# Channel mixer: the first products get priority over the second products everywhere, and attention runs 15 instead of 18 units ahead

## Chip, cores, metric

One core of a Trainium2 chip. The metric is the device time of one execution in microseconds, lower is better. A kernel is run several times and the median is quoted. Ratios are the mean time of one kernel's fast runs over the mean of the other's fast runs of the same rounds, so they are not quite the ratio of the quoted medians.

## The reference

Attention with a block mask, then a ResMLP block on its output. The matrices that matter here:

```python
# 4 batches, 8 heads, 768 tokens, head size 64, so d_model = 512; all scaled and masked as usual
x   = attention(q, k, v, mask)            # (4, 768, 512)
a1  = alpha1 * x + beta1
u   = x + lam * einsum('ts,bsd->btd', w_tok, a1)          # token mixer
a2  = alpha2 * u + beta2
out = u + lam * (maximum(a2 @ w_ch1, 0) @ w_ch2)          # channel mixer, 512 -> 2048 -> 512
```

`a2 @ w_ch1` are the *first products*, the product with `w_ch2` the *second products*. `lam` is about 0.01.

## The kernel before

The kernel is written as a list of jobs. A small list scheduler runs while the program is built. It puts each job on an engine in the order that its own estimates suggest, and that order is then fixed: every engine works through its list and waits wherever its next instruction isn't ready. So a job's priority (its third argument, the smaller the earlier) changes no work, only the order of instructions.

```python
# this kernel's PSUM buffers, in banks: sps 2 x 2 (scores), mm 2 x 1, cp 1, ops 1
slots = dict(sps=2, mm=2, cp=1, ops=1, eT=NET, head=NQB, vext=NV, ld=NLD, rel=3, ...)

for kk in range(2 * B):                       # a half batch (384 tokens) each
    relus = []
    for f in range(16):                       # first products: 16 groups of 4 matmuls, 384 columns
        # c1: hp[:, 0:384] += w1b[:, dk, f-th 128].T @ uT[:, dk, half]    for dk in 0..3
        # rl: hts[kk][:, f, :] = relu(hp + b1)  on ACT or DVE; frees the mm buffer
        deps = [ut_jobs[b * NPAIR + n] for n in range(NPAIR)] + b1_jobs
        take = ((("mm", "sps"), ("mmsel", kk, f)),) + (("hts",) if f == 0 else ())
        j = Job("PE", mmt(4, HS), (5, kk, f), c1, deps, take=take, ...)
        jr = Job(("ACT", "DVE"), 600.0, (0, kk, f), rl, [j], give=(("mmsel", kk, f),))
        relus.append(jr)
    for mi, (m, lo, w) in enumerate(parts):   # second products: per 128 tokens 4 pieces of 4 matmuls
        for r in range(4):
            deps = relus[4 * r : 4 * r + 4] + w2_jobs[2 * r : 2 * r + 2] + ([prev] if prev else [])
            take = ... ("cp", "ops") ...      # one accumulator; ops and sps only after attention
            prev = Job("PE", mmt(4, w), (6 if kk == 2 * B - 1 else 4, kk, mi, r), c2, deps, take=take, ...)
        # otf (DVE): ot = x_sb + cp, frees cp;  store (SP): ot to memory
...
def gated(j):      # a score job may run at most LEAD units ahead of the channel mixer;
                   # a unit is one of the nine steps in which a head pair's scores are made
    return j.gate is not None and j.gate >= NS and j.gate - NS > st["ch"] / rate + LEAD
...
if e == "PE" and not st["ch2"]:
    fill(t - free_at[e] - 60.0)               # until the first second product: filler matmuls in planned holes
```

Also on TensorE are the scores (of the first six head pairs one head at a time, later two heads of 64 rows at once), the value products into the bank `ops`, and the token mixer into `mm`. On DVE are the normalisation of each head (`x_sb`, which frees `ops`), masking, the copies of v (`vext`), and the additions.

The softmax here doesn't subtract the row's maximum and nothing guards it: scores larger than these inputs give would overflow.

## Time and profile before

| | before |
|---|---|
| median of 4 runs | 318.59 us (318.51 to 319.05) |
| span in the profile | 317.3 us |
| PE / DVE / ACT busy | 97% / 66% / 64% |
| last matmul ends | 313.8 us |

In the views PE stands for TensorE's matmuls and PEld for its weight loads, DVE for VectorE, ACT for ScalarE, POOL for GpSimd and SP for the engine that issues stores and transposing DMAs; PEclk is the clock granted to TensorE in 40 slices of the time, where 9 means 90% of full speed or more. From the page of the kernel before, first the busy time of the engines and the granted clock, then groups of instructions: line, engine, operation, output and inputs, shapes, count, then busy us, mean ns of one, idle us before them.

```profile
PE 307.4 (97%) x3234; PEld 189.6 (60%) x3269; DVE 208.8 (66%) x432; ACT 204.6 (64%) x262; POOL 51.2 (16%) x91
...
PEclk9999999999999999999999999999999999999999
...
L973 ACT ACTIVATE hts<-mm,b1t 128x384 bf16<-128x384 f32 x92 | 53.6, 583 | 59.8 <-PE mm L962 57.3
L962 PE MATMUL mm<-uT,w1b 128*128 128x384 bf16 x472 | 90.5, 326 | 0.6
L1007 PE MATMUL cp<-w2b,hts 128*128 128x512 bf16 (+1 forms) x307 | 75.8, 373 | 1.5
...
L977 DVE TENSOR_SCALAR hts<-mm,b1t 128x384 bf16<-128x384 f32 x26 | 16.0, 617 | 14.5 <-PE mm L962 14.5
```

ACT waits for TensorE's first products (57 us), not the other way round: TensorE is full. But 97% busy says little about what is left to win. A first product "takes" 326 ns on the page, and yet in the trace one starts every 162 ns. Products overlap, so a hole of 0.2 us between two of them shows up as hardly any idle time (0.6 us for all of L962). The holes have to be read from the start times of single records. Here are those around 122 us, where three groups of first products stand in a row (start in us, then the distance to the next start in ns):

```
122.127  163     second group
122.290  162
122.452  436     <- 274 ns longer than the others
122.888  162     third group, into the mm buffer that the first group used
123.050  162
```

The timeline of the kernel before around that place (start, duration, engine and line, out<-in, count):

```profile
121.31 2.39 PE L962 MATMUL mm<-uT,w1b 128*128 128x384 bf16 x12
121.35 1.02 ACT L780 ACTIVATE eT<-sps 128x1024 f16<-128x1024 f32 x1
...
122.25 1.15 ACT L973 ACTIVATE hts<-mm,b1t 128x384 bf16<-128x384 f32 x2
```

The first group ends its stream at 121.97. Its ReLU starts only at 122.25, behind an exponential, and takes 0.58 us. Until it has read the buffer the third group can't start. Ten such places after 85 us cost 0.10 to 0.27 us each, together 2.04 us. In all ten the first product of the held group starts 49 to 52 ns after the end of a ReLU; seven of these ReLUs run on DVE and three on ACT.

What PE itself waits for, in the view of waits of the kernel before (us in total, times, longest):

```profile
PE cp L171 <- DVE warm L166: 1.2, 1, 1.2
PE ops L716 <- DVE x_sb L651: 1.0, 1, 1.0
PE sps L676 <- ACT eT L691: 0.6, 1, 0.6
PE sps L676 <- ACT qx L238: 0.5, 1, 0.5
PE mm L427 <- DVE kx L281: 0.4, 1, 0.4
```

All but the second lie in the first 45 us, ahead of anything that the change touches. The second is at 69 us; the timeline there (in brackets: idle time before it and what ended it):

```profile
69.26 0.36 DVE L834 COPY vext<-v 128x768 f16<-128x768 f16 x1 [1.21 <-DMA v<-in_v_dram]
...
69.54 0.19 DVE L648 RECIPROCAL rcp<-ops 128x6 f32<-128x6 f32 x1
69.76 0.56 DVE L651 TENSOR_TENSOR x_sb<-ops,rcp 128x384 f32<-128x384 f32 x1
...
70.38 0.54 PE L716 MATMUL ops<-vext,eT 128*128 128x65 f16 x12 [1.00 <-DVE x_sb L651]
```

DVE's list has the copy of the eighth pair's v ahead of a normalisation that was ready. The v load landed late, DVE stood still for 1.2 us, and TensorE paid 1.0 us. (The view of waits counts from modelled ends and shows a little less than the start times do: this wait is 1.17 us by them.)

One more caution in reading: some matmul records are missing from this trace (3234 are there). A gap that is exactly one product longer than usual (216 ns before a second product) is a missing record, not a wait.

### The profile page before, as it was taken

The numbers are of one execution on the slowest core, as the hardware profiler recorded it, in microseconds if no ns is written. First come the engines' busy times: TensorE is split into PE (matmuls) and PEld (weight loads), VectorE is DVE, ScalarE is ACT, GpSimd is POOL, SyncE is SP. The second block draws the span as 40 slices with busy tenths as digits, with TensorE's granted clock in tenths as the row PEclk, the third lists the DMA queues.
The fourth block names the chain that finished last, engine by engine and source line by source line (L and its number), as shares of the span: only waits on it lengthen the run. The fifth ranks groups of instructions, "written<-read, shape, count | busy, mean of one in ns | idle before, by whom it ended". The sixth has DMA issues, their size and how long they took to land.

```text
span 317.3 us, 7694 instructions
## 1 busy us (share of the span) xinstructions
PE 307.4 (97%) x3234; PEld 189.6 (60%) x3269; DVE 208.8 (66%) x432; ACT 204.6 (64%) x262; POOL 51.2 (16%) x91
## 2 busy tenths in 40 slices
PE   7999999989999999999999999999999999999995
PEld 3677868865655555555656565555656565555544
DVE  4558988978778786978888786878777650201001
ACT  4999889987785666656765667657775526253620
POOL 4647170000221121122131121120000000000000
PEclk9999999999999999999999999999999999999999
DMA  6999999991544865436454744346100300201001
GB/s 148 184 254 201 211 202 215 176 161 30 78 73 74 140 72 95 84 77 116 62 92 82 135 81 89 75 82 110 28 3 33 92 8 19 101 0 66 35 33 66
DMA packets 47210, 30.81 MB, mean 97 GB/s; under 512 B 27552, under 2 KB 43080, under 8 KB 47176
## 3 DMA queue, kind: packets, MB, share of 16 engines
q0 software_dynamic: 15984, 15.47, 31.1%
q1 hardware_dynamic: 30940, 14.61, 20.5%
q8 instruction: 25, 0.41, 0.5%
q10 hardware_dynamic: 252, 0.24, 0.3%
q14 instruction: 9, 0.07, 0.1%
HBM read 32.04 MB, written 6.33 MB: 121 GB/s over the span
## 4 chain that ended last, share of the span: by engine, by line
PE 74%; DMA 13%; issue 5%; POOL 4%; DVE 2%; ACT 1%; POOLq 0%
PE mm L962 23%; PE cp L1007 22%; DMA v<-in_v_dram 9%; PE ops L812 8%; PE sps L754 7%; PE mm L889 7%; PE ops L1007 4%; DMA wtk<-in_moe_w_tok_dram 3%; PE sps L962 2%; POOL k L317 1%; DVE hts L977 1%; POOL q L317 1%; DMA q2f<-in_q_dram 1%; POOL v L317 1%; POOL w2b L390 1%
## 5 line engine op out<-in xcount | busy, mean ns | idle before, releaser
L780 ACT ACTIVATE eT<-sps 128x1024 f16<-128x1024 f32 x90 | 88.3, 1020 | 29.2 <-PE sps L754 28.3
L973 ACT ACTIVATE hts<-mm,b1t 128x384 bf16<-128x384 f32 x92 | 53.6, 583 | 59.8 <-PE mm L962 57.3
L962 PE MATMUL mm<-uT,w1b 128*128 128x384 bf16 x472 | 90.5, 326 | 0.6
L1007 PE MATMUL cp<-w2b,hts 128*128 128x512 bf16 (+1 forms) x307 | 75.8, 373 | 1.5
L785 DVE TENSOR_TENSOR eT<-eT,maskT 128x1024 f16<-128x1024 f16 x90 | 60.6, 686 | 13.2 <-ACT eT L780 12.8
L962 PEld LDWEIGHTS <-w1b 128*128 128x128 bf16 x512 | 47.2, 98 | 35.4 <-issue 5.1
L1007 PEld LDWEIGHTS <-hts 128*128 128x128 bf16 x400 | 36.6, 98 | 33.3 <-issue 0.3
L691 ACT ACTIVATE eT<-sps 128x1024 f16<-128x1024 f32 (+1 forms) x55 | 52.3, 1016 | 4.6 <-PE sps L676 4.3
L1024 DVE TENSOR_TENSOR ot<-x_sb,cp 128x512 f32<-128x512 f32 (+1 forms) x21 | 14.1, 673 | 44.9 <-PE cp L1007 40.6
L812 PEld LDWEIGHTS <-eT 128*128 128x128 f16 x720 | 29.1, 97 | 16.3 <-issue 5.9
L889 PE MATMUL mm<-a1p,wtokT 128*128 128x128 bf16 x576 | 36.8, 219 | 0.0
L812 PE MATMUL ops<-vext,eT 128*128 128x65 f16 x720 | 35.2, 194 | 0.0
L889 PEld LDWEIGHTS <-wtokT 128*128 128x128 bf16 x576 | 33.3, 98 | 2.2
L676 PE MATMUL sps<-qx,kx 88*128 88x512 bf16 (+1 forms) x144 | 31.5, 324 | 1.3 <-ACT eT L691 0.6
L315 POOL COPY held<-flag 1x1 bf16<-1x1 bf16 x24 | 8.3, 348 | 137.6 <-DVE flag L335 137.6
L754 PE MATMUL sps<-qx,kx 64*128 64x512 bf16 (+1 forms) x240 | 27.3, 326 | 0.0
L977 DVE TENSOR_SCALAR hts<-mm,b1t 128x384 bf16<-128x384 f32 x26 | 16.0, 617 | 14.5 <-PE mm L962 14.5
L716 PEld LDWEIGHTS <-eT 128*128 128x128 f16 x432 | 19.0, 97 | 6.7 <-DVE x_sb L651 1.7
L716 PE MATMUL ops<-vext,eT 128*128 128x65 f16 x432 | 21.0, 193 | 1.0 <-DVE x_sb L651 1.0
L899 DVE TENSOR_TENSOR x_sb<-x_sb,mm 128x384 f32<-128x384 f32 x32 | 17.6, 551 | 5.5 <-PE mm L889 5.4
L651 DVE TENSOR_TENSOR x_sb<-ops,rcp 128x384 f32<-128x384 f32 x32 | 17.8, 557 | 1.1
L905 DVE TENSOR_TENSOR ub<-x_sb,a_bc 128x384 bf16<-128x384 f32 x32 | 17.3, 553 | 0.2
(71 smaller groups left out, 226.6 us busy)
## 6 DMA issues: line engine op xcount, KB each, us to landing
out_dram<-ot SPq DMA_DIRECT2D x23, 256.0 KB
v<-in_v_dram POOLq DMA_DIRECT2D x16, 192.0 KB, 5.0
q<-in_q_dram POOLq DMA_DIRECT2D x15, 192.0 KB, 3.6
k<-in_k_dram POOLq DMA_DIRECT2D x15, 192.0 KB, 4.0
w1b<-in_moe_w_ch_dram POOLq DMA_DIRECT2D x4, 512.0 KB, 10.2
w2b<-in_moe_w_ch_dram POOLq DMA_DIRECT2D x4, 512.0 KB, 13.2
wtk<-in_moe_w_tok_dram POOLq DMA_DIRECT2D x3, 384.0 KB, 10.4
maskT<-mask_rows SPq DMA_DIRECT2D x14, 72.0 KB
```

Of the source, the lines that this page charges most:

```text
L676: nc.tensor.matmul(sps[:, f - u * UN : f - u * UN + w], kx[h][0:KC, ts(jt, P)], qx[h][0:KC, c : c + w], start=True, stop=True,)
L691: nc.scalar.activation(eT[:, c], sps[:, c], AF.Exp, bias=EXPB, scale=SCALE)
L716: nc.tensor.matmul(ops[p, a][:, t * VW : t * VW + D + 1], eTs[p, u][:, ts(i - u * GU, P)], vx[:, a, jt, 0 : D + 1], start=(i % HT == 0), s ...
L754: nc.tensor.matmul(sps[:, a * 512 + lo : a * 512 + lo + w], kx[sl][r, ts(jt, P)], qx[sl][r, c : c + w], start=True, stop=True,)
L780: nc.scalar.activation(eT[:], sps[:], AF.Exp, bias=EXPB, scale=SCALE)
L785: nc.vector.tensor_tensor(out=e, in0=e, in1=maskT[:, u, :].unsqueeze(1).broadcast_to([P, 2, 512]), op=ALU.min,)
L812: nc.tensor.matmul(ops[p, a][:, t * VW : t * VW + D + 1], eTs[p, u][:, a * 512 + c * P : a * 512 + (c + 1) * P], vx[:, a, jt, 0 : D + 1], ...
L889: nc.tensor.matmul(tp[:, j, :], wtokT[:, s, ts(3 * g + j, P)], tl["a1p", p][:, s, :], start=(s == 0), stop=(s == NT - 1),)
L962: nc.tensor.matmul(hp[:, 0:HS], w1b[:, dk, ts(f, P)], uTs[b][:, dk, ts(hf, HS)], start=(dk == 0), stop=(dk == 3),)
L973: nc.scalar.activation(hts[kk][:, f, :], hp[:, 0:HS], AF.Relu, bias=b1t[:, f : f + 1], scale=1.0)
L977: nc.vector.tensor_scalar(out=hts[kk][:, f, :], in0=hp[:, 0:HS], scalar1=b1t[:, f : f + 1], scalar2=0.0, op0=ALU.add, op1=ALU.max,)
L1007: nc.tensor.matmul(cps[kk, mi][:, 0:w], hts[kk][:, nk, ts(m, P)], w2tile[0][:, nk, lo : lo + w], start=(nk == 0), stop=(nk == 15),)
```

## The change

Second products shall only fill spots in which TensorE would wait. First products keep priority 5, and all second products get 6; before, that held only for the last half batch, and the others had 4. Attention's lead over the channel mixer goes from 18 to 15 units.

```diff
-LEAD = 18
+LEAD = 15
@@ first products
             deps = [ut_jobs[b * NPAIR + n] for n in range(NPAIR)] + b1_jobs
+            if f:
+                deps.append(first)
             ...
             j.ch = True
+            if not f:
+                first = j
@@ second products
-                prev = Job("PE", mmt(4, w), (6 if kk == 2 * B - 1 else 4, kk, mi, r), c2, deps, take=take,
+                prev = Job("PE", mmt(4, w), (6, kk, mi, r), c2, deps, take=take,
```

The dependency on `first` makes sure that the group that takes the `hts` buffer comes first. Built without it, the changed kernel failed in the scheduler (a ReLU looked for a buffer that didn't exist yet).

## The prediction

> **What bounds the kernel.** TensorE, by streaming. The page has PE busy 97% of 317.3 us, which alone proves little: it counts filler products, and the Trainium skill ("Trainium Kernel Development and Optimization", Performance Expectations) calls matmul busy time a bad metric because matmuls are pipelined. I read start-to-start times from the trace's matmul records: 162 ns for 384 columns, 216 for 512, 56 for 128. The skill's "TensorE: Matmul & The Clock Gate" (section on 56 ns, not 53.3) gives columns / 2.4 GHz + about 2.5 ns: 162.5, 215.8, 55.8. The trace agrees, clock granted 1.0. From 71 us to the last product (313.8 us) TensorE streams almost without a hole. The waits view has PE matmuls waiting 3.7 us in total. Entering and leaving a 64-row score block costs about 96 + 93 ns, 45 times, in both orders.
>
> Holes after 60 us: (a) ten of 0.10 to 0.27 us, 2.0 us in sum, where a third first product in a row needs one of two "mm" PSUM buffers whose ReLU isn't done (650 ns per group; ReLU 583 ns on ACT, 617 on DVE, plus drain); (b) 1.0 us at 69.4 us: a value product held by a normalisation that stood behind a late v load (DVE waited 1.2 us for it); (c) fillers of 0.1 to 0.4 us between 63 and 76 us. Other gaps are exactly one product long (216 ns): missing records.
>
> **What changes.** Matmuls, ReLUs and additions are the same but one filler (47 becomes 46, about 0.2 us). Only order moves: first products earlier, second ones as filler; attention held to 15, not 18, units ahead. ACT (64%) and DVE (66%) have slack off the critical path.
>
> **Costed from the two instruction orders and the pitches above.** Products that need an mm buffer freed less than 0.8 us of TensorE work before: 11 before, 4 after. At 0.22 us each (0.1 at milder ones) waits fall from 2.0 to 0.8 us: gain 1.2 to 1.5. Filler: gain 0.2. The wait at 69 us: 18 mixing products now stand ahead of it, but the late v load still delays DVE: gain 0 to 0.5. Against it: second products share one cp bank during attention, freed by a 0.67 us addition after the drain. Between two groups the old order left at least 1.29 us; the new leaves 0.75 twice and 1.04 once: loss 0.5 to 0.9. After the last token mix 28 second products (6.0 us) cover the path to the transposed u, which took 3.5 us before (mix ended 259.0, transpose packets 262.5): no wait. The tail, last product, addition, store, 3.5 us, is the same.
>
> Sum: gain 0.9 to 1.5 us, less unknown mismatches. **Predicted 317.3 us, 80% range 316.0 to 318.9.** Faster by over 2% (below 312.3): 0.01. Within 2%: 0.97. Slower: 0.02. The reordering has about 3 us of holes to win, under 1%, where TensorE is full.
>
> **What would show it.** ReLU holes: at most 1 us in gaps between first products, nearly all before 85 us. cp holes: two of 0.2 to 0.5 us where a second product starts a new cp group, near 120 and 190 us. Summed pitch unchanged within 0.5 us. Last matmul near 312.5 us; PE still 97%.
>
> **What would make it wrong.** Waits not seen in the order: DVE behind the planned order (ReLU or additions late), score blocks starving ACT, or the late v load becoming a longer stall at 70 us: each could add 1 to 3 us. A win over 3 us would mean that I misread missing records for streaming.

## The result

| | before | after |
|---|---|---|
| median of 4 runs each | 318.59 us (318.51 to 319.05) | 318.08 us (317.68 to 318.22) |
| ratio, 95% interval | | 0.9979 (0.9962 to 0.9996) |
| span in the profile | 317.3 us | 315.9 us |
| last matmul ends | 313.8 us | 312.4 us |

The lines of the page of the kernel after that answer to those of before:

```profile
PE 308.5 (98%) x3268; PEld 189.3 (60%) x3268; DVE 211.7 (67%) x441; ACT 199.3 (63%) x253; POOL 51.3 (16%) x91
...
PEclk9999999999999999999999999999999999999999
...
L962 PE MATMUL mm<-uT,w1b 128*128 128x384 bf16 x468 | 88.4, 326 | 0.3 <-DVE x_sb L899 0.2
L973 ACT ACTIVATE hts<-mm,b1t 128x384 bf16<-128x384 f32 x82 | 47.7, 582 | 51.7 <-PE mm L962 49.9
L1011 PE MATMUL cp<-w2b,hts 128*128 128x512 bf16 (+1 forms) x320 | 76.9, 374 | 0.2
...
L977 DVE TENSOR_SCALAR hts<-mm,b1t 128x384 bf16<-128x384 f32 x35 | 21.5, 615 | 17.8 <-PE mm L962 17.7
```

Nothing costs more or less by itself. Nine ReLUs moved from ACT to DVE (those into `mm` on DVE go from 26 to 35), which is the scheduler's doing. The waits of PE in the kernel after:

```profile
PE cp L171 <- DVE warm L166: 1.2, 1, 1.2
PE sps L676 <- ACT qx L238: 0.6, 1, 0.6
PE sps L676 <- ACT eT L691: 0.6, 1, 0.6
PE mm L427 <- DVE kx L281: 0.4, 1, 0.4
PE mm L427 <- DMA wtk<-in_moe_w_tok_dram: 0.3, 1, 0.3
PE mm L962 <- DVE x_sb L899: 0.2, 1, 0.2
```

The 1.0 us wait of value products is gone from this trace; 0.2 us before a first product (at 71 us) is new. From the start times, three ReLU waits are left (0.22, 0.10 and 0.22 us at 83, 87 and 90 us), and none after 95 us.

A new kind of wait appears: a second product that starts a new accumulation in the one `cp` bank waits for DVE's addition to read the old one. The timeline of the kernel after at 127 us shows how close it is:

```profile
126.83 0.69 DVE L1028 TENSOR_TENSOR ot<-x_sb,cp 128x512 f32<-128x512 f32 x1 [0.30 <-PE cp L1011]
126.84 0.11 PEld L754 LDWEIGHTS <-kx 64*128 64x128 bf16 x4
126.84 0.60 PE L754 MATMUL sps<-qx,kx 64*128 64x512 bf16 x4
...
127.57 1.02 PE L1011 MATMUL cp<-w2b,hts 128*128 128x512 bf16 x4
```

DVE's addition ends at 127.52 and the next second product starts 0.05 us later, which gives the wait away. The score block of four matmuls before it stood for 725 ns from its start to the next product, where such blocks elsewhere take 538 ns, the 92 ns of leaving the block included. So 0.19 us was waited here. The same happens at 197 us.

### The profile page after: what moved, and what is told of

It reads as the page before. It is cut to its first block, busy times and chain, and to the rows that moved or that the text cites. A ratio compares the mean times of both kernels' runs of the same rounds, so it can differ in the third digit from the quotient of the medians.

```text
span 315.9 us, 7725 instructions
## 1 busy us (share of the span) xinstructions
PE 308.5 (98%) x3268; PEld 189.3 (60%) x3268; DVE 211.7 (67%) x441; ACT 199.3 (63%) x253; POOL 51.3 (16%) x91
## 4 chain that ended last, share of the span: by engine, by line
PE 75%; DMA 16%; issue 3%; DVE 3%; POOL 3%; POOLq 0%
PE mm L962 24%; PE cp L1011 21%; DMA v<-in_v_dram 10%; PE ops L812 8%; PE sps L754 7%; PE mm L889 7%; PE ops L1011 5%; DMA wtk<-in_moe_w_tok_dram 3%; PE sps L962 2%; DMA k<-in_k_dram 2%; DMA q2f<-in_q_dram 1%; POOL k L317 1%; POOL q L317 1%; POOL v L317 1%; DVE ot L1028 1%
## 5 line engine op out<-in xcount | busy, mean ns | idle before, releaser
L962 PE MATMUL mm<-uT,w1b 128*128 128x384 bf16 x468 | 88.4, 326 | 0.3 <-DVE x_sb L899 0.2
L973 ACT ACTIVATE hts<-mm,b1t 128x384 bf16<-128x384 f32 x82 | 47.7, 582 | 51.7 <-PE mm L962 49.9
L1011 PE MATMUL cp<-w2b,hts 128*128 128x512 bf16 (+1 forms) x320 | 76.9, 374 | 0.2
L962 PEld LDWEIGHTS <-w1b 128*128 128x128 bf16 x512 | 46.5, 97 | 32.4 <-issue 4.6
L1028 DVE TENSOR_TENSOR ot<-x_sb,cp 128x512 f32<-128x512 f32 (+1 forms) x20 | 13.4, 671 | 37.0 <-PE cp L1011 36.8
L889 PE MATMUL mm<-a1p,wtokT 128*128 128x128 bf16 x576 | 36.1, 219 | 0.1
L977 DVE TENSOR_SCALAR hts<-mm,b1t 128x384 bf16<-128x384 f32 x35 | 21.5, 615 | 17.8 <-PE mm L962 17.7
L754 PEld LDWEIGHTS <-kx 64*128 64x128 bf16 x240 | 8.0, 94 | 16.5 <-issue 14.1
```

Of the source, the lines that this page charges most:

```text
L754: nc.tensor.matmul(sps[:, a * 512 + lo : a * 512 + lo + w], kx[sl][r, ts(jt, P)], qx[sl][r, c : c + w], start=True, stop=True,)
L889: nc.tensor.matmul(tp[:, j, :], wtokT[:, s, ts(3 * g + j, P)], tl["a1p", p][:, s, :], start=(s == 0), stop=(s == NT - 1),)
L962: nc.tensor.matmul(hp[:, 0:HS], w1b[:, dk, ts(f, P)], uTs[b][:, dk, ts(hf, HS)], start=(dk == 0), stop=(dk == 3),)
L973: nc.scalar.activation(hts[kk][:, f, :], hp[:, 0:HS], AF.Relu, bias=b1t[:, f : f + 1], scale=1.0)
L977: nc.vector.tensor_scalar(out=hts[kk][:, f, :], in0=hp[:, 0:HS], scalar1=b1t[:, f : f + 1], scalar2=0.0, op0=ALU.add, op1=ALU.max,)
L1011: nc.tensor.matmul(cps[kk, mi][:, 0:w], hts[kk][:, nk, ts(m, P)], w2tile[0][:, nk, lo : lo + w], start=(nk == 0), stop=(nk == 15),)
```

## Experiments

Twelve runs in three calls. The runs of each call shared one chip and the runs of the kernel before (11 per call; medians 319.08, 318.93 and 319.39 us). In the texts, A and its rivals are:

- A: the change gains what it takes out of TensorE's ReLU waits, plus, at most, part of the stall at 69 us.
- B: the gain is luck of the profiled runs and of the late v load.
- C: the lead makes the gain, not the priority.
- D: a stall taken away at 69 us only moves.
- E: the "ReLU waits" aren't the ReLU's time.
- F: a late DVE at 69 us is handed on at full price.

They speak of nine ReLU waits in places. There are ten. They also give each `cp` wait at 127 and 197 us as 0.09 us, and 0.45 us for all waits on DVE there and at 253 to 255 us. That took off the cost of leaving a score block twice: the start times give 0.19 us each and 0.64 us in all.

### 1. Both kernels again

No edit.

> The kernel before, unchanged, for a second trace. Theory A (the change gains what it takes out of TensorE's ReLU waits): after 75 us the same ten waits of 0.1 to 0.27 us between first products, 2.0 to 2.3 us in sum, since they follow from the order. Rival B (the gain is luck of the profiled runs and of the late v load): the waits or the 1.0 us stall at 69 us differ from run to run by as much as the gain. Time ratio to before 1.000 within 0.001 under both; the 69 us stall decides: A needs it within 0.3 us of 1.0, B lets it be anything from 0 to 1.5.

Measured: 319.37 us, ratio 0.9992 (0.9960 to 1.0023). The ten ReLU waits again, 2.04 us, each within 4 ns of its value in the first trace. The stall at 69 us was 0.6 instead of 1.0 us in the view of waits.

> The kernel after, unchanged, with five rounds and a second trace. A: 0.9975 to 0.9985 of before (about 0.6 us), ReLU waits under 1 us in sum, all before 95 us, and about 0.2 to 0.3 us of cp waits near 127, 197 and 254 us. B: ratio 0.999 to 1.0005, with another sum of waits in this trace than in the first.

Measured: 317.84 us, ratio 0.9948 (0.9920 to 0.9977). The waits that follow from the order were those of the first trace: 0.22, 0.10 and 0.22 us of ReLU, 0.19 us at 127 and again at 197 us, and at 253 to 255 us one of 0.18 and one of 0.09 us. At 70 us there was no wait at all. The same kernel pair that gave 0.9979 gave 0.9948 here, a larger gain than A's range, although all waits that follow from the order stayed. In the traces two things vary: the place at 69 to 70 us, and the start, which the change doesn't touch (the first product of the token mixer starts between 30.06 and 30.65 us). Part of rival B is true, but not its main claim.

### 2. The two parts alone

```diff
 lead_only:    before, with LEAD = 15
 prio_lead18:  after, with LEAD = 18
```

> The kernel before with the lead of attention cut from 18 to 15 units and nothing else. Nine places with an mm buffer freed under 0.8 us of TensorE work before, against 11 before and 4 after, no cp spot under 0.75 us beyond two. A: ReLU waits 1.4 to 1.9 us, so 0.2 to 0.6 us of gain at most: ratio 0.998 to 1.000. Rival C (the lead makes the gain, priority none): ratio equal to that of after, waits too.

Measured: 320.04 us, ratio 1.0027 (0.9993 to 1.0061). My expectation, a small gain, was wrong in both halves. The ReLU waits fell further than to the 1.4 to 1.9 us expected, from 2.04 to 0.65 us in four places, but 3.0 us of others came in: value products that wait for a masked exponential on DVE (0.42 us, twice), second products that wait for DVE's addition (0.43 us twice, 0.19 once), the token mixer waiting at three places (0.43, 0.18 and 0.18 us), and three waits of 0.11 us before first products. My reading, which no run tests: with second products done as soon as possible, no stock of them is left to put where DVE is late.

> The kernel after with the lead put back to 18: priority alone. Seven places under 0.8 us for mm buffers, all before 82 us, and four cp spots of 0.75 us plus one of 1.04. A: ReLU waits 0.9 to 1.4 us, cp waits 0.3 to 0.5 us, ratio 0.9975 to 0.9995. C: ratio 1.000, nothing gained without the lead.

Measured: 318.16 us, ratio 0.9959 (0.9930 to 0.9989). ReLU waits 0.63 us, all before 95 us, below the range of 0.9 to 1.4; waits for the `cp` bank 0.61 us at four places, above the range of 0.3 to 0.5; one value product waits 0.18 us; the stall at 69 us is there (1.1 us). So the priority takes out the ReLU waits by itself, without the new waits that the lead alone brings, and C falls: the lead alone takes out as many but gains no time. The ratio can't be told from that of the full change (0.9948). What the lead adds to the priority stands in the orders: the kernel after and lead_only have 18 more products of the token mixer ahead of the value product that stalls at 69 us, and 46 filler matmuls; prio_lead18 and the kernel before have neither (47 fillers). So the lead, and not the priority, works on the stall.

### 3. The late v load

```diff
+        if p == 7:
+            putv[p].deps.append(norm[5, 0])
```

The copy of v now stands behind the normalisation in DVE's list. In the kernel before, the scheduler also answered with another order on TensorE: 18 more products of the token mixer now stand ahead of the value product that stalled, beside smaller shifts. In the kernel after they stood there already, and TensorE's order is unchanged.

> The kernel before, but DVE copies the eighth pair's v only after the first normalisation of the sixth pair, so that this normalisation no longer stands behind the late v load. The order of TensorE changes only between 67 and 71 us. Theory A (the change gains from two places: the ReLU waits, about 1.3 us, and the stall at 69 us, 0.7 to 1.2 us): the stall at 69 us falls from 0.7 to 1.2 us to under 0.4 us, the nine ReLU waits (2.0 us) stay, ratio to before 0.9965 to 0.9985, so about half of the change's gain. Rival D (the stall only moves: what DVE misses at 69 us TensorE waits for a little later): other waits of as much appear between 70 and 80 us and the ratio is 0.999 to 1.001.

Measured: 318.49 us (318.14 to 318.69), ratio 0.9977 (0.9962 to 0.9991). The stall at 69 us is gone and no other came in its place; the ten ReLU waits stayed at 2.04 us. The view of waits of PE in this run has those of the first 45 us and nothing else. But the trace shows that here it is the order on TensorE that covers DVE:

```profile
69.78 1.17 PE L891 MATMUL mm<-a1p,wtokT 128*128 128x128 bf16 x18
...
70.08 0.56 DVE L651 TENSOR_TENSOR x_sb<-ops,rcp 128x384 f32<-128x384 f32 x1
...
71.23 0.95 PE L716 MATMUL ops<-vext,eT 128*128 128x65 f16 x26
```

DVE was late in this run too: a k load held it for 1.5 us, and the normalisation ended at 70.64 us. In the old order the value product would have stood where the 18 mixing products start, at 69.78 us, and would have waited about 0.9 us (an estimate from these times). So D falls for the edit as a whole, but that moving the copy alone would end the stall isn't shown. The spread of the six runs is 0.55 us, where the eleven of the kernel before spread over 1.7 us. That points to the place at 69 us as the source of most of its scatter, through late loads on DVE, of which v is one.

> The same edit on the kernel after; the order of TensorE there is unchanged. A: its stall at 70 us was 0.3 us in one trace and none in the other, so at most 0.3 us is gained: 0.993 to 0.9985 of before, equal to after within 0.1%. Its four ReLU waits (0.77 us) stay. D: waits move within 70 to 80 us, no gain.

Measured: 317.36 us (317.04 to 317.63), ratio 0.9945 (0.9929 to 0.9961). This pair of runs is the cleanest comparison of the change, since neither stalls at 69 us: 318.49 against 317.36, 1.13 us or 0.35%. The traces account for most of it, in us:

| | before with the edit | after with the edit |
|---|---|---|
| ReLU waits | 2.04 (10 places) | 0.55 (3 places) |
| filler matmul at 75 us | 0.22 | none |
| token mixer at 78 us, waits for DVE's `a1p` addition | none | 0.22 |
| value and second product at 253 to 255 us, wait for DVE | none | 0.27 |
| second products at 127 and 197 us, wait for `cp` | none | 0.37 |
| sum | 2.26 | 1.41 |

The difference is 0.85 us. From the start of the first products to the end of the last product the two traces take 246.79 and 245.95 us, which is 0.84 us less, so nothing of size is missing from the table. The times differ by 1.13 us; the runs of each kernel spread over 0.55 to 0.59 us, and the two profiled runs also differ by 0.6 us before 31 us, which isn't the change's doing.

### 4. Shorter ReLUs

```diff
-  nc.scalar.activation(hts[kk][:, f, :], hp[:, 0:HS], AF.Relu, ...)
+  nc.scalar.activation(hts[kk][:, f, 0 : 2 * P], hp[:, 0 : 2 * P], AF.Relu, ...)   # DVE's likewise
-  hts[kk][:, nk, ts(m, P)],
+  hts[kk][:, nk, ts(min(m, 1), P)],                                               # wrong on purpose
```

The order of instructions is unchanged on all engines. (The comparison with the reference still passed. That says only that the channel mixer's share of the output, scaled by `lam`, is small against the tolerance.)

> The kernel before with each ReLU cut from 384 to 256 columns and the third second product reading the second's columns again: wrong on purpose, same order of instructions on every engine. A (the waits are the time in which a ReLU holds its mm buffer): a ReLU becomes 100 to 140 ns shorter, each of the nine waits shrinks by that, so their sum falls from 2.03 to 0.7 to 1.1 us, and the time by 0.9 to 1.3 us, ratio 0.996 to 0.998. Rival E (the waits come from an exponential ahead of the ReLU in ACT's queue, or from the drain): the waits stay at 1.8 to 2.0 us, ratio 0.999 to 1.001.

Measured: 317.67 us, ratio 0.9970 (0.9935 to 1.0006), the interval wide because one of the six runs took 321.33 us; the other five lie between 317.17 and 318.11. The ReLUs, by group (ACT, then DVE):

```profile
L973 ACT ACTIVATE hts<-mm,b1t 128x256 bf16<-128x256 f32 x92 | 43.6, 474 | 67.6 <-PE mm L962 66.5
L977 DVE TENSOR_SCALAR hts<-mm,b1t 128x256 bf16<-128x256 f32 x26 | 12.6, 483 | 14.3 <-PE mm L962 14.3
```

They are 109 and 134 ns shorter. The typical wait of 0.22 us became 0.09, the two of 0.27 became 0.08, the two of 0.10 vanished: 0.68 us in sum after 85 us instead of 2.04, a little below the range of 0.7 to 1.1. So it is the time for which a ReLU holds its `mm` buffer, and E falls as the main cause. The sum can be read at 87 us in the first trace: the ReLU on DVE starts 0.20 us after the end of its group's stream, takes 0.62 us, and the product follows 0.05 us later, 0.87 us in all, of which the next group's stream covers 0.65. The exponential ahead of the ReLU adds only the 0.05 us by which the two longest waits exceed the others.

The run of 321.33 us was the profiled one, and it shows one way in which a single run becomes slow. This is the table by stretches for PE and the clock (PE, PEld, DVE, ACT and POOL busy with counts, PEclk, DMA share, GB/s):

```profile
70.20:72.20 2.00, 0.43 (x2) 0.00 (x0) 1.33 (x5) 1.02 (x1) 0.00 (x0) 1.00 1.30 203
72.20:73.20 1.00, 0.89 (x18) 0.75 (x19) 1.00 (x3) 0.00 (x0) 0.00 (x0) 1.00 1.19 246
73.20:74.90 1.70, 1.70 (x23) 1.70 (x22) 1.70 (x4) 1.02 (x1) 0.00 (x0) 0.50 0.08 18
74.90:76.70 1.80, 1.80 (x18) 1.40 (x17) 1.11 (x3) 0.00 (x0) 0.00 (x0) 0.52 0.00 0
```

Late q, k and v loads stretched the stall: 0.6 us of waiting at 68 us, then 1.7 us at 70 us. About 1 us after TensorE had resumed, its granted clock fell to 0.50 for 3.41 us. The slowest runs of the kernel before (321.30 and 320.97 us) aren't of this kind: their granted clock is 0.999, where this run has 0.994. They have no trace.

> The same cut on the kernel after, wrong on purpose. A: its ReLU waits (0.77 us in four places) fall to 0.25 to 0.4 us, so cheaper ReLUs gain only 0.3 to 0.6 us here against 0.9 to 1.3 in the kernel before: the gap between the two kernels with short ReLUs is smaller by 0.5 to 0.9 us than with full ones. The cp waits near 127, 197 and 254 us (0.45 us) stay. E: as much gained or as little as in the kernel before.

Measured: 317.65 us, ratio 0.9958 (0.9940 to 0.9977). ReLU waits 0.18 us in two places. The fourth place, 0.22 us at 79 us, did not move: it is no ReLU wait but the token mixer waiting for DVE's `a1p` addition, so the after kernel had three ReLU waits (0.55 us) and not four (0.77). With short ReLUs the two kernels have medians of 317.67 and 317.65 us. The gap of about 1.1 us is gone, where I expected it to shrink by 0.5 to 0.9 us and the ReLU waits to stay above 0.25. The waits that follow from the order agree: 0.90 us before (0.68 of ReLU, 0.22 of filler) and 1.04 us after (0.18 of ReLU, 0.22 of the token mixer, 0.64 of the others), so no gap is left. The times alone don't prove it, since this profiled run of the kernel after also stalled for nearly 1 us at 70 us.

### 5. How DVE's delay at 69 us is paid, and the best version again

```diff
-            nc.vector.tensor_tensor(out=x_sb[...], in0=op[...], in1=rcp[...], op=ALU.mult)
+            for _ in range(3 if (p, a) == (5, 0) else 1):
+                nc.vector.tensor_tensor(out=x_sb[...], in0=op[...], in1=rcp[...], op=ALU.mult)
```

> The kernel before with the first normalisation of the sixth pair done three times over (same result, same orders): DVE late by 0.9 to 1.2 us more at the place where TensorE stalled for 0.7 to 1.2 us. Theory F (this place hands a late DVE on to TensorE at full price, which is what the late v load does too): the stall becomes 1.7 to 2.4 us and the time grows by 0.9 to 1.2 us; if the stall reaches about 1.8 us or more the granted clock halves for about 3.4 us and another 1.7 us are lost, as in the one slow run of the short-ReLU kernel. Rival D (the slack behind it absorbs it): under 0.4 us.

Measured: 321.46 us, ratio 1.0063 (1.0031 to 1.0096), in two kinds of runs: 319.99 and 320.60 us, and 322.32 and 322.46 us. The profiled run is one of the slow kind. Its wait, and its clock in stretches of 2 us (columns as above):

```profile
PE ops L717 <- DVE x_sb L652: 2.2, 1, 2.2
```

```profile
71.00:73.00 2.00, 1.02 (x15) 0.91 (x16) 1.97 (x5) 0.00 (x0) 0.00 (x0) 0.80 0.57 117
73.00:75.00 2.00, 2.00 (x22) 1.73 (x21) 1.66 (x3) 1.02 (x1) 0.00 (x0) 0.50 0.04 8
75.00:77.00 2.00, 2.00 (x27) 1.40 (x24) 1.11 (x2) 0.26 (x1) 0.00 (x0) 0.84 0.00 0
```

DVE's delay of about 1.1 us (two normalisations of 0.56) became about 1.2 us more of waiting than the 1.0 us in the first trace, and in this run the clock halved for 3.41 us, in which 1.7 us of work are lost. F holds for the kernel before. The two faster runs (0.6 and 1.2 us over the median of before) escaped the clock drop: they have no trace, but the record gives each run's granted clock, 1.0 for these two and 0.995 for the two slower ones. So with the same delay the clock fell in two runs of four, and the runs give no threshold for it.

> The same on the kernel after, in which 18 more mixing products (1.0 us) stand ahead of the held value product. F: the stall at 70 us becomes 0.9 to 1.4 us, so time grows by 0.7 to 1.2 us over after, and the clock holds: after loses as much per us of DVE but starts 0.8 us better. D: under 0.4 us.

Measured: 319.08 us, ratio 0.9986 (0.9960 to 1.0011), 1.1 us over the kernel after. The wait at 70 us was 1.4 us and the clock stayed at 1.0. The change doesn't absorb a late DVE, but TensorE reaches the held product 0.57 us later, since 18 matmuls of the token mixer (56 ns each) now stand ahead of it and two score matmuls (216 ns each) behind. So the same delay of DVE made a wait of 1.4 us here (and 0.3 us before the first product that follows) and of 2.2 us in the kernel before. The rest of the difference is these two runs': here the copy of v began 0.1 us earlier and TensorE's first products 0.15 us later.

> The kernel after, unchanged, beside the next run on one chip. Expected again 0.993 to 0.998 of before. Theory A: the ReLU and cp waits are the same to 10 ns as in its two traces (0.77 us, and 0.27 us near 254 us, beside two hidden ones of 0.09 us); only the wait at 70 us may differ (0 to 0.5 us).

Measured: 318.00 us (317.24 to 320.16), ratio 0.9966 (0.9936 to 0.9995). The waits that follow from the order repeated to 6 ns. At 70 us this trace has the stall (0.7 us, then 0.3 us before a first product), because the v copy on DVE began at 69.92 us, against 68.83 and 68.65 us in the two earlier traces: more than the 0 to 0.5 us I had written.

> The best version so far: the change, and the copy of the eighth pair's v behind the first normalisation of the sixth pair. Expected 0.993 to 0.996 of before and 0 to 0.6 us under the kernel after of the same rounds; runs spread over less than 0.7 us, since no wait hangs on the late v load. If its gain over after (0.5 us across two calls) was the chip's, the two are equal here.

Measured: 317.62 us (317.29 to 317.73), ratio 0.9945 (0.9928 to 0.9962), with a spread of 0.44 us against 2.9 us for the kernel after. It gave 0.9945 in both calls, while the change alone gave 0.9979, 0.9948 and 0.9966. (The spread of the kernel after isn't always wide: in the first experiments it was 0.43 us.) This is the best version that was run: it beats the kernel before clear of noise, and the kernel after by 0.4 us in the medians and mainly by its steadiness. The ratio between those two was not taken on its own, so I don't call it a proven gain in the mean.

## Why the prediction was right

The time, 318.08 us, lies in the range of 316.0 to 318.9, and "within 2%" was right. The centre of 317.3 was 0.8 us low. Point by point:

- **TensorE is full, so only about 3 us can be won.** Right. After 95 us and up to the last product, the kernel before with all its records has only its ReLU waits as holes, and the change turned a possible 3 us into about 1.
- **ReLU waits fall from 2.0 to 0.8 us.** Right in mechanism (shorter ReLUs shrink exactly these waits). They fell to 0.55 us; the remaining 0.22 us that I had counted as ReLU is a wait of the token mixer for DVE, so the sum of 0.8 us came out right partly by luck. They lie before 91 us rather than 85.
- **Filler: 0.2 us.** Right, one matmul of 216 ns.
- **Stall at 69 us: gain 0 to 0.5 us.** Not a bound: in the first two pairs of traces the gain was 0.8 and 0.6 us. Nor did I see the place for what it seems to be, the main source of scatter. The 0.57 us by which TensorE comes later is a gain only while DVE is late there, and of that 0.3 us can come back as a first product's wait. In five traces that keep the two orders it was 1.0 and 0.6 us before, 0.2, 0 and 1.0 us after.
- **`cp` waits: loss 0.5 to 0.9 us, near 120 and 190 us.** Right in mechanism, at the low end in size. They are at 127 and 197 us and cost 0.19 us each, just under the 0.2 to 0.5 us I had given. The 0.75 us of TensorE work reckoned between two accumulations is what the trace has (0.76 us, from 126.63 to 127.38 us). At 253 to 255 us the cost was 0.27 us together, of which 0.18 is a value product that waits for a normalisation, which I had not foreseen. In all 0.64 us, inside the range partly because of that unforeseen wait.
- **Transposed u covered, tail unchanged.** Right: no wait there; the last matmul is 3.5 us before the end in both.

What made the timed gain (about 0.6 us) smaller than the difference of the two profiled spans (1.4 us) was the choice of runs: the profile of before is of a run of 319.08 us, above the median of its runs by 0.5 us, and that of after is of the fastest run of its four (317.68 us). From the start of the first products on, the two traces differ by 1.70 us: 0.85 by the order, as in the table, and 0.85 at 69 to 71 us by the start times. With that place out of the way the change gains 0.85 us by the traces and 1.1 us by the times. Without it, the prediction's own sum is 0.5 to 1.2 us (1.4 to 1.7 gained, 0.5 to 0.9 lost), so the sum was right and not only the range.

Open: why DVE can copy this v at 68.7 us in one run and only at 71.2 us in another. It stands behind the loads of `w2b` in POOL's list, but no run moved it. Open too is how much of the scatter is v's alone: only in the kernel after was the copy of v moved with TensorE's order unchanged, and there the spread without it was 0.4 us and 2.9 us.

## What to carry to other kernels

When one engine is full, a new order can win only the holes in that engine's stream: count them from start times of single instructions, since busy shares of a pipelined engine hide holes of 0.2 us. A stock of work that needs no scarce buffer, kept back to fill exactly the spots where the next product would wait for a buffer, takes most of them away; what it can't cover is another engine that stands behind a late load in its own fixed list, so put an instruction that waits for a load behind those that free somebody's buffer. Compare profiles only after taking a second one of each kernel: waits that follow from the order repeat to a few ns, and the rest is the run's luck.

## What the Trainium skill lacked or had wrong

- "TensorE: Matmul & The Clock Gate", in the sections on the clock gate, on oscillation and on why it matters, has the clock fall after an idle window of about 3.4 us and advises to avoid idle gaps of over about 3 us. Here a wait of 2.2 us was enough in one run, and waits of 0.6 and 1.7 us about 2 us apart in another; 1.4 us was not. The length of the slow phase, 3.41 us at 0.50, agrees with the page's window. Its spacing of products in the section on 56 ns, not 53.3 (columns / 2.4 GHz + 2.5 ns), agrees too: 162, 216 and 56 ns.
- The same page, Part 3, says that weight loads overlap running matmuls only where the row group differs (its Part 2 also allows a background buffer, and so does Part 3 itself under its heading on the mechanism). In these traces loads of about 98 ns before products of the same 128 rows are hidden completely (162 ns from start to start), and it is the switch from 128 rows to 64 that shows: 96 ns on entering a score block and 92 to 93 ns on leaving it, 45 times. "TensorEngine Tiling (Array Packing)" says only that changing the tiling mode drains TensorE; no page gives a time for such a switch.
- "Trainium Kernel Development and Optimization", Performance Expectations, is right that matmul busy time is a bad measure, but names MFU and the busy share of weight loads as the good ones. That share was 60% in both kernels, while TensorE's stream had no holes but the few listed: start-to-start times told what neither busy share did.
